# Two attention and mixer layers at decode: order of heads at the change of layer, the path from one layer's rows to the next layer's queries, and the end of the kernel

## The chip, the cores and the metric

One core of a Trainium2 chip runs the whole program; the other cores are idle. The metric is the device time of one execution in microseconds, as a median of several runs. A profiled execution of the same program gives the trace that the views below are taken from.

## The reference

Two sequences (B = 2), one new token each, of width D = 512. A layer is grouped-query attention over a cache of 32,768 keys with 32 query heads on 8 key and value heads of width 128, and then a mixer block whose MLP runs along the token axis (there is one token, so each of the 512 channels is sent through 1,792 hidden values by itself). Both are added to x after a LayerNorm. Two such layers follow each other, with the same weights and the same cache. All is float32.

```python
def _A_ref(x, k_cache, v_cache, wq, wo):
    q = (x @ wq).reshape(B, Sq, Hq, Dh).transpose(0, 2, 1, 3)
    k = jnp.repeat(k_cache, rep, axis=1)
    v = jnp.repeat(v_cache, rep, axis=1)
    scores = jnp.einsum("bhqd,bhkd->bhqk", q, k) * (Dh ** -0.5)
    p = _softmax(scores, axis=-1)
    o = jnp.einsum("bhqk,bhkd->bhqd", p, v)
    return o.transpose(0, 2, 1, 3).reshape(B, Sq, Hq * Dh) @ wo

def _B_ref(x, w1, b1, w2, b2):
    h = _layernorm(x, axis=-1)
    u = _gelu(jnp.einsum("bsd,sf->bdf", h, w1) + b1)
    y = jnp.einsum("bdf,fs->bds", u, w2) + b2
    return y.transpose(0, 2, 1)

x = x + _A_ref(_layernorm(x, axis=-1), A_k_cache, A_v_cache, A_wq, A_wo)
x = x + _B_ref(_layernorm(x, axis=-1), B_w1, B_b1, B_w2, B_b2)
# and the same two lines once more
```

The second layer's queries for a sequence need that sequence's first layer to be complete: all eight heads, the output projection, the mixer and a LayerNorm. Its keys and values are those of the first layer again.

## The kernel before

A unit is one layer, sequence and key head, (layer, b, h). There are 32 units, each with 64 cells of K and 64 of V. A cell is a tile of 128 partitions by 512 floats, 256 KiB. The on-chip buffer `mem` holds 105 cells (`CELLS`), so nearly everything is streamed, and the two layers stream the same cache twice. Work goes in steps of four cells. A K step runs eight matmuls (two per cell in float32) into score tiles in PSUM (`k_step`, line 315); a V step runs eight matmuls into `acc` (`v_step`, line 366).

Class `Order` (line 41) writes down the order of all K and V steps. In the steady part it is K of one unit and then V of the unit before, so that the softmax of a unit is done while V of its predecessor passes. At each of the two changes of layer (one per sequence) stand three units: x, the last head of layer 0 for that sequence; fill, a unit of the other sequence that keeps the machine busy while the mixer of x's sequence is worked out; and y, the same head as x in layer 1, which needs its result. The order there is K of x, V of the unit before, first half of K of fill, V of x, second half of K of fill, V of fill, K of y, V of y. Because y reads the same cache as x, 64 V cells and 8 K cells of x are kept on chip for y (`KEPT_V`, `KEPT_K`). With 16 cells of weights for the two heads concerned, 17 cells are left for streaming during that time.

`plan_loads` (line 112) plans all loads ahead of time with a model of the queue and of TensorE (`CELL_US`, `LAND_US`, `LEAD_US`, `STEP_US`, and the `us` of the hooks): for each load it takes the largest of 32, 24, 16, 8 or 4 cells that makes the queue wait least, and a place in `mem`. `Order.cut` fixes sizes by hand: four-cell loads for the second half of fill's K and for all of fill's V, a taper (16, 8, 4, 4) at the end of x's V, and (16, 8, 4, 2, 1, 1) at the end of the last unit's V. All loads are issued from SP (line 722), each waiting until the last matmul that reads its cells has ended.

Everything else hangs on steps: `at(p, f, ...)` (line 627) runs f behind step p, in the order of TensorE's queue. For each unit these are the maximum of the scores (`max_1`, `max_2`), the transposes and exponentials, the denominators, `take_out` (copy `acc` to SBUF), `out_1` (sum the four row groups and divide) and `out_2` (output projection into `rows`). When a sequence's last unit of a layer has passed, the mixer follows: `mix_1` (broadcast x into PSUM), `take_rows`, `mix_2` (add the attention output, LayerNorm statistics), `hidden_tiles` in eight turns (two Gelu tiles on ScalarE and the projection of the two before), `take_rows`, `mix_4` (add the mixer output, statistics of the next LayerNorm), `to_columns` (line 535) and the queries of y in three pieces (`make_q`). At a change this chain runs from one step behind x's V to 22 steps behind it, and K of y begins two steps later.

The last unit has its own end, `last_mixer` (line 547): its last two cells (`THIN`) go to `acc` by thin matmuls that need no summing over row groups, and the mixer's Gelu runs as three direct tiles and then groups of 3, 3, 3 and 2 tiles, whose affine part VectorE has made. The output leaves in four transfers, two each from SP and ScalarE.

## Time and profile before

| | |
|---|---|
| median of 3 runs | 2521.4 us (2520.32 to 2522.16) |
| the profiled execution | 2520.16 us, span 2518.4 us |
| mean granted TensorE clock | 0.753 of full speed |
| TensorE busy with matmuls | 1442.3 us (57% of the span) |
| VectorE, ScalarE | 181.3 us, 183.7 us (7% each) |
| DMA | 1066.71 MB, 424 GB/s on the mean, 236 transfers issued from SP, most of 1, 2, 4 and 8 MB |

The page of the profile gives the busy time of each engine, a row of 40 slices of the span with the rate of the DMA engines, and the chain of work that ended last, followed back from the end. `SPq` is SP's queue of DMA issues. In the rows of windows the columns are the stretch, its length, busy time and number of instructions of PE (TensorE matmul), PEld (weight loads), DVE (VectorE), ACT (ScalarE) and POOL (GpSimd), then the granted clock of TensorE as a part of full speed, the busy share of the DMA engines and GB/s. In rows of the timeline they are start, duration, engine, line, operation, output <- input, shapes and count; in brackets stands the idle time before, and what ended it.

### The profile page before, as it was taken

How to read it: one execution, taken by the hardware profiler on the slowest of the kernel's cores; microseconds unless marked ns; L12 is line 12 of the kernel's file. 1: busy time of each engine (PE TensorE's matmuls, PEld its weight loads, DVE VectorE, ACT ScalarE, POOL GpSimd, SP SyncE). 2: the span in 40 equal slices, each digit the busy share in tenths (PEclk: the TensorE clock that was granted, in tenths of full speed). 3: DMA queues.
4: the chain of work that ended last, by engine and by line, in shares of the span. 5: the costliest groups of instructions: out<-in, count | busy, mean ns of one | idle time of the engine just before them, and what ended most of it. 6: DMA issues, size and time to landing. Idle time of an engine off the chain costs nothing.

```text
span 2518.4 us, 20745 instructions
## 1 busy us (share of the span) xinstructions
PE 1442.3 (57%) x9484; PEld 400.0 (16%) x9484; DVE 181.3 (7%) x473; ACT 183.7 (7%) x572; POOL 4.9 (0%) x16
## 2 busy tenths in 40 slices
...
GB/s 416 432 436 434 434 431 432 431 431 431 431 433 433 433 435 433 418 435 396 403 427 398 397 425 430 438 434 431 431 433 433 434 430 438 434 426 433 426 430 258
DMA packets 33792, 1066.71 MB, mean 424 GB/s; under 512 B 4005, under 2 KB 4009, under 8 KB 4394
## 3 DMA queue, kind: packets, MB, share of 16 engines
...
q10 hardware_dynamic: 6, 0.00, 0.0%
HBM read 1065.38 MB, written 0.00 MB: 423 GB/s over the span
## 4 chain that ended last, share of the span: by engine, by line
DMA 67%; PE 31%; ACT 1%; DVE 1%; issue 0%; SPq 0%; POOLq 0%; ACTq 0%; DVEq 0%
DMA mem<-in_kt_dram 36%; DMA mem<-in_v_dram 30%; PE acc L375 12%; PE scores L322 12%; PE misc L420 2%; PE rows L437 2%; PE misc L289 1%; ACT S L357 0%; PE rows L493 0%; PE misc L346 0%; PE misc L340 0%; PE bcast L457 0%; PE acc L592 0%; PE misc L539 0%; PE bcast L519 0%
## 5 line engine op out<-in xcount | busy, mean ns | idle before, releaser
L375 PE MATMUL acc<-mem,S 128*16 128x512 f32 x4092 | 626.7, 711 | 523.0 <-DMA mem<-in_v_dram 513.3
L322 PE MATMUL scores<-mem,qz 128*32 128x512 f32 x4096 | 613.4, 734 | 524.9 <-DMA mem<-in_kt_dram 524.8
L357 ACT ACTIVATE S<-S,neg 128x128 f32<-128x128 f32 x256 | 129.6, 509 | 2247.1 <-DVE S L352 1180.9
L322 PEld LDWEIGHTS scores<-mem,qz 128*32 128x32 f32 x4096 | 136.8, 128 | 926.0 <-DMA mem<-in_kt_dram 469.2
L375 PEld LDWEIGHTS acc<-mem,S 128*16 128x16 f32 x4092 | 129.9, 106 | 848.3 <-issue 793.1
L332 DVE TENSOR_REDUCE mx<-scores 128x1 f32<-128x512 f32 x64 | 44.3, 692 | 827.9 <-PE scores L322 827.9
L289 PE MATMUL misc<-mem,xn 128*2 128x512 f32 (+1 forms) x144 | 86.9, 737 | 4.3 <-DMA mem<-in_wqo_dram 4.3
L420 PEld LDWEIGHTS misc<-selg,row 128*128 128x128 f32 x256 | 50.8, 295 | 46.8 <-issue 41.6
L352 DVE STREAM_TRANSPOSE S<-scores 128x512 f32<-128x512 f32 x64 | 45.5, 711 | 140.7 <-PE acc L375 140.7
L420 PE MATMUL misc<-selg,row 128*128 128x4 f32 x256 | 53.6, 333 | 0.6 <-DVE row L405 0.6
L437 PE MATMUL rows<-mem,oT 128*1 128x512 f32 x248 | 52.1, 931 | 0.0
L357 ACT ACTIVATION_READ_ACCUMULATOR S<-S,neg 128x1 f32 x256 | 47.7, 187 | 0.0
L493 PE MATMUL rows<-hid,cols_sb 128*1 128x512 f32 x84 | 33.8, 616 | 1.0 <-ACT hid L508 1.0
L342 DVE TENSOR_REDUCE m<-misc 1x4 f32<-1x128 f32 x32 | 8.9, 278 | 342.4 <-PE misc L340 342.4
L415 DVE COPY row<-acc 128x512 f32<-128x512 f32 x31 | 21.5, 692 | 149.7 <-PE acc L375 149.7
L508 ACT ACTIVATE hid<-bcast,bias,scale 128x512 f32<-128x512 f32 x42 | 30.4, 774 | 17.0 <-PE rows L493 8.6
L289 PEld LDWEIGHTS misc<-mem,xn 128*2 128x2 f32 (+1 forms) x144 | 14.5, 101 | 74.2 <-issue 72.9
L428 DVE TENSOR_TENSOR oT<-misc,rl 128x4 f32<-128x4 f32 x32 | 5.2, 162 | 283.6 <-PE misc L420 283.6
L294 DVE COPY row<-misc 2x512 f32<-2x512 f32 (+1 forms) x18 | 12.2, 679 | 183.5 <-PE misc L289 123.0
L340 PE MATMUL misc<-ident,mxa 128*1 128x128 f32 x64 | 17.8, 375 | 5.1 <-DVE mxa L338 5.1
L401 DVE RECIPROCAL rl<-misc 128x4 f32<-128x4 f32 x32 | 5.9, 183 | 197.4 <-PE misc L399 197.4
L298 PEld LDWEIGHTS misc<-ident,row 2*128 2x128 f32 (+1 forms) x144 | 17.3, 186 | 16.2 <-issue 12.7
...
## 6 DMA issues: line engine op xcount, KB each, us to landing
mem<-in_kt_dram SPq DMA_DIRECT2D x27, 2048.0 KB, 13.0
...
mem<-in_wqo_dram SPq DMA_DIRECT2D x14, 2048.0 KB, 33.1
...
mem<-in_v_dram SPq DMA_DIRECT2D x8, 2048.0 KB, 10.4
...
```

Of the source, the lines that this page charges most:

```text
L289: nc.tensor.matmul(q_ps[us][:n, :], xn[layer][:, d, b : b + n], wq[:, d, :], start=(d == 0), stop=(d == DT - 1))
L322: nc.tensor.matmul(sc_ps[u, half][32 * row : 32 * row + 32, :], qz[:, at : at + 32], cells(at_cell["K", u, g], 1), start=(i == 0), stop=(i ...
L332: nc.vector.tensor_reduce(mx[u][:, half : half + 1], sc_ps[u, half], axis=AX.X, op=ALU.max)
L340: nc.tensor.matmul(pm[:1, :P], mxa, ident, start=True, stop=True)
L352: nc.vector.transpose(S[half], sc_ps[u, half])
L357: nc.scalar.activation(s[:, :, h], s[:, :, h], AF.Exp, bias=neg[u][:, h : h + 1], scale=SCALE, accum_out=lsum[u][:, half, h : h + 1],)
L375: nc.tensor.matmul(acc[32 * row : 32 * row + R * QT, :], S[half][:, col : col + R * QT], vc, start=(g < NG), stop=(g >= quads - NG),)
L415: nc.vector.tensor_copy(asb[u], acc)
L420: nc.tensor.matmul(po[:, :R], asb[u][:, t * DH : (t + 1) * DH], selg[:, t * R : (t + 1) * R], start=(t == 0), stop=(t == QT - 1),)
L437: nc.tensor.matmul(rows[b][32 * r : 32 * r + 1, :], oT[u][:, r : r + 1], wo_of(u)[:, r, :], start=(u == order.first_of[layer, b]), stop=(u ...
L493: nc.tensor.matmul(rows[key[1]][32 * g : 32 * g + 1, :], w2c[:, f : f + 1], hid.pop((key, f)), start=(f < NG), stop=(f >= FT - NG),)
L508: nc.scalar.activation(hid[key, f], px[key], AF.Gelu_apprx_tanh, bias=shift[key][:, f : f + 1], scale=slope[key][:, f : f + 1],)
```

## The change

The order at a change becomes K of x, V of the unit before, all of K of fill, V of x, V of fill, K of y, V of y. Ten K cells are kept instead of eight, and `mem` has 106 cells; the room comes from the second buffer of `hidden`, whose place the row tile takes for every other hidden tile. The planner's constants for landing and lead are 1.1 and 1.8 us.

The chain from x's V to y's queries is rewritten for the 16 steps of fill's V. `mix_1` runs two steps before V of x ends, `out_1` and `out_2` directly behind it. `half_way` turns the rows of the attention into columns while the mixer runs, and `change_1` adds the columns of the mixer's rows. The queries are computed from x without its LayerNorm, beside a second row that holds the column sums of the weights; the mean and the deviation come from two all-partition sums, and `change_2` applies both with a pair of factors in the small matmuls that turn the queries into columns. `mix_4`'s copy and statistics and `to_columns` go.

At the end of the kernel eight cells are thin instead of two, and they go to a PSUM tile of their own, so that `take_out` and the summing of the row groups (`out_sum`) run before the last four cells. `last_rows` puts what is known of the rows into PSUM before the last V starts, where the denominators, the row copy and `mix_1` now stand as well. The two halves of the last projection lie in different PSUM tiles, copied out by VectorE and ScalarE; one broadcast and one `bn_stats` follow. The last Gelu groups are 3, 3, 3, 1, 1, and the output leaves in one transfer. The first half of the last unit's V is loaded in two pieces. At the start, x and the small columns are loaded from ScalarE's queue instead of SP's.

```diff
-CELLS = 105
+CELLS = 106
 WCELLS = 8
-KEPT_K = 8
+KEPT_K = 10
 KEPT_V = 64
 SIZES = (32, 24, 16, 8, 4)
 FINAL = (16, 8, 4, 2, 1, 1)
 TAPER = (16, 8, 4, 4)
-THIN = 2
+THIN = 8
 SLOTS = 4
 DIRECT = 3
-TAIL_GROUPS = (3, 3, 3, 2)
-TAIL_CELLS = 16
+TAIL_GROUPS = (3, 3, 3, 1, 1)
+TAIL_CELLS = 18
 EPS = 1e-5
 
 LOAD_US = 0.12
 CELL_US = 0.6024
-LAND_US = 1.0
-LEAD_US = 2.5
+LAND_US = 1.1
+LEAD_US = 1.8
 STEP_US = 1.44
...
-        self.k(x0), self.v(before[-1]), self.k(fill0, 0), self.v(x0), self.k(fill0, 1), self.v(fill0)
-        self.k(y0), self.v(y0), self.k(x1), self.k(fill1, 0), self.v(x1), self.k(fill1, 1), self.v(fill1)
+        self.k(x0), self.v(before[-1]), self.k(fill0), self.v(x0), self.v(fill0)
+        self.k(y0), self.v(y0), self.k(x1), self.k(fill1), self.v(x1), self.v(fill1)
         self.k(y1), self.v(y1), self.k(n)
...
-        for x, fill, _ in self.changes:
+        for x, fill, y in self.changes:
+            self.cut("K", y, KEPT_K, (-KEPT_K % STEP,))
             self.cut("V", x, HALF, TAPER)
-            self.cut("K", fill, HALF, (STEP,) * 8)
             self.cut("V", fill, 0, (STEP,) * 16)
+        self.cut("V", self.last, 0, (HALF // 2, HALF // 2))
         self.cut("V", self.last, HALF, FINAL)
...
-    hidden = ctx.enter_context(tc.tile_pool(name="hidden", bufs=2))
+    hidden = ctx.enter_context(tc.tile_pool(name="hidden", bufs=1))
...
-    nc.sync.dma_start(xcols, x)
+    nc.scalar.dma_start(xcols, x)
...
-                    acc[32 * t : 32 * t + R, :DH],
+                    thin[32 * t : 32 * t + R, :DH],
                     S[half][:, col + t * R : col + (t + 1) * R],
                     vc[:, t * DH : (t + 1) * DH],
-                    start=False,
-                    stop=True,
-                    skip_group_check=True,
+                    start=(g == quads),
+                    stop=(g == 2 * HALF - 1),
...
+    thin = rows[0]
+    po_of = {}
+
+    def out_sum(u):
+        po_of[u] = pmisc.tile([P, G], F32, name="misc")
         for t in range(QT):
             nc.tensor.matmul(
-                po[:, :R],
+                po_of[u][:, :R],
                 asb[u][:, t * DH : (t + 1) * DH],
                 selg[:, t * R : (t + 1) * R],
                 start=(t == 0),
-                stop=(t == QT - 1),
-            )
+                stop=(t == QT - 1 and u != order.last),
+            )
+
+    def out_1(u):
+        if u == order.last:
+            nc.tensor.matmul(po_of[u][:, :R], asb["thin"], selg[:, :R], start=False, stop=True)
+        else:
+            out_sum(u)
+        po = po_of[u]
...
-                hid[key, f] = hidden.tile([P, D], F32, name="hid")
+                hid[key, f] = hidden.tile([P, D], F32, name="hid") if f % 2 else row_tile()
...
+    def all_sum(dst, src):
+        p = pmisc.tile([P, G], F32, name="misc")
+        nc.tensor.matmul(p[:, :DT], ones, src, start=True, stop=True)
+        nc.vector.tensor_reduce(dst, p[:, :DT], axis=AX.X, op=ALU.add)
+
+    def columns(key):
         pt = pmisc.tile([P, G], F32, name="misc")
         for d in range(DT):
             nc.tensor.matmul(
-                pt[:, d : d + 1], ysb[key][:, d * P : (d + 1) * P], ident[:, :1], start=True, stop=True
-            )
-        xT[b] = const.tile([P, DT], F32, name=f"xT_{b}")
-        nc.vector.tensor_scalar_add(xT[b], pt[:, :DT], b2c)
-        mv, rs = stats[key]
-        nc.vector.tensor_scalar(xn[1][:, :, b], pt[:, :DT], mv[:, 0:1], rs, op0=ALU.subtract, op1=ALU.mult)
+                pt[:, d : d + 1], ysb[key][:, d * P : (d + 1) * P], selg[:, 0:1], start=True, stop=True
+            )
+        return pt[:, :DT]
+
+    def half_way(key):
+        nc.vector.scalar_tensor_tensor(sq, columns(key), b2c, xT[key[1]], op0=ALU.add, op1=ALU.add)
+
+    def change_1(key, y):
+        b = key[1]
+        x = xq[b][:, :, 0]
+        wq = wq_sb[0, y[2]]
+        nc.vector.tensor_add(x, columns(key), sq)
+        xT[b] = x
+        q_ps[y] = pfix.tile([P, G], F32, name="bcast")
+        for d in range(DT):
+            nc.tensor.matmul(q_ps[y][:2, :], xq[b][:, d, :], wq[:, d, :], start=(d == 0), stop=(d == DT - 1))
+        all_sum(negm, x)
+        nc.vector.tensor_scalar_mul(negm, negm, -1.0 / D)
+        nc.vector.tensor_scalar_add(xn[1][:, :, b], x, negm)
+        nc.vector.tensor_mul(sq, xn[1][:, :, b], xn[1][:, :, b])
+        q_row[y] = row_tile()
+        nc.scalar.activation(q_row[y][:2, :], q_ps[y][:2, :], AF.Copy)
+
+    def change_2(key, y):
+        b = key[1]
+        all_sum(spread, sq)
+        nc.vector.tensor_scalar(spread, spread, 1.0 / D, EPS, op0=ALU.mult, op1=ALU.add)
+        nc.gpsimd.tensor_tensor(spread, spread, half_neg, op=ALU.pow)
+        nc.vector.scalar_tensor_tensor(
+            pair, ident[:2, 1:2], negm[:2, :], ident[:2, 0:1], op0=ALU.mult, op1=ALU.add
+        )
+        nc.vector.tensor_scalar_mul(pair, pair, spread[:2, :])
+        pt = pmisc.tile([P, G], F32, name="misc")
+        for r in range(R):
+            nc.tensor.matmul(
+                pt[:, r : r + 1], q_row[y][:2, r * DH : (r + 1) * DH], pair, start=True, stop=True
+            )
+        q_out((y,), pt)
+        nc.vector.tensor_scalar_mul(xn[1][:, :, b], xn[1][:, :, b], spread)
+
+    rest = [None, None]
+
+    def last_rows(u):
+        layer, b, h = u
+        key = (layer, b)
+        y = ysb[key]
+        nc.tensor.matmul(px[key], sel1, y, start=False, stop=False, skip_group_check=True)
+        for g in range(NG):
+            to = rows[b][32 * g : 32 * g + 1, :P]
+            nc.tensor.matmul(to, xT[b][:, g : g + 1], ident, start=True, stop=False, skip_group_check=True)
+            nc.tensor.matmul(
+                to, selg[:, 0:1], y[:, g * P : (g + 1) * P], start=False, stop=False, skip_group_check=True
+            )
+        for k in range(2):
+            rest[k] = pscore.tile([P, G], F32, name="scores")
+            nc.vector.memset(rest[k][:, : D // 2], 0.0)
...
     def last_mixer(u):
...
+        tiles = [cells(tail_at + k, 1) for k in range(TAIL_CELLS)]
+        flat, y, few = tiles[FT + 1], tiles[FT + 2], tiles[FT + 3][:, :DH]
         p = px[key]
-        st = work.tile([P, 2, 6], F32, name="ln_st2", bufs=1)
+        st = work.tile([P, 6], F32, name="ln_st")
         mv = work.tile([P, 2], F32, name="ln_mv")
         rs = work.tile([P, 1], F32, name="ln_rs")
+        nc.vector.tensor_copy(few, thin[:, :DH])
+        asb["thin"] = few
+        out_1(u)
         for k in range(2):
             for r in range(R):
                 nc.tensor.matmul(
-                    rw[32 * r : 32 * r + 1, k * w : (k + 1) * w],
+                    rest[k][32 * r : 32 * r + 1, :w],
                     oT[u][:, r : r + 1],
                     wo_of(u)[:, r, k * w : (k + 1) * w],
-                    start=False,
+                    start=True,
                     stop=True,
-                    skip_group_check=True,
                 )
-        halves_copy(y, rw)
-        for k in range(2):
-            c = slice(k * w, (k + 1) * w)
-            nc.tensor.matmul(p[:, c], sel1, y[:, c], start=False, stop=True, skip_group_check=True)
-            nc.vector.bn_stats(st[:, k, :], p[:, c])
-        res = acc[:, :P]
+        nc.vector.tensor_copy(y[:, :w], rest[0][:, :w])
+        nc.scalar.activation(y[:, w:], rest[1][:, :w], AF.Copy)
+        nc.tensor.matmul(p, sel1, y, start=False, stop=True, skip_group_check=True)
+        nc.vector.bn_stats(st, p)
+        res = rows[b][:, :P]
         for g in range(NG):
-            c = slice(g * P, (g + 1) * P)
-            to = acc[32 * g : 32 * g + 1, :P]
-            nc.tensor.matmul(to, xT[b][:, g : g + 1], ident, start=True, stop=False, skip_group_check=True)
-            nc.tensor.matmul(to, selg[:, 0:1], y[:, c], start=False, stop=False, skip_group_check=True)
+            nc.tensor.matmul(
+                rows[b][32 * g : 32 * g + 1, :P],
+                selg[:, 0:1],
+                y[:, g * P : (g + 1) * P],
+                start=False,
+                stop=False,
+                skip_group_check=True,
+            )
...
-        for g in range(NG):
-            (nc.sync if g % 2 else nc.scalar).dma_start(
-                out[b : b + 1, g * P : (g + 1) * P], o[32 * g : 32 * g + 1, :]
-            )
+        nc.sync.dma_start(out[b : b + 1, :].rearrange("o (g c) -> (o g) c", g=NG), o[0 : P : P // NG, :])
...
-        at(v_mid + 2, denominators, u, us=0.2)
-        at(v_end, take_out, u)
+        at(v0 - 1 if u == order.last else v_mid + 2, denominators, u, us=0.4)
         if u == order.last:
-            at(v_mid + 4, gelu_table)
-            at(v_mid + 3, mix_1, key, us=0.8)
-            at(v_end, out_1, u)
+            at(v0 - 1, take_rows, key)
+            at(v0 - 1, table, AF.Gelu_apprx_tanh)
+            at(v0 - 1, mix_1, key)
+            at(v0 - 1, last_rows, u)
+            at(v_end - 2, take_out, u)
+            at(v_end - 1, out_sum, u)
             at(v_end, last_mixer, u)
             continue
-        at(v_end + 1, out_1, u, us=1.0)
-        at(v_end + 2, out_2, u, us=2.4)
-        if u == order.last_of[key]:
-            e = v_end
-            at(e + 1, mix_1, key, us=0.8)
-            at(e + 3, take_rows, key)
-            at(e + 4, mix_2, key, us=0.7)
-            g0 = e + 9
-            for k in range(FT // 2 + 1):
-                at(g0 + k, hidden_tiles, key, k, us=1.0)
-            g0 += FT // 2
-            at(g0 + 1, take_rows, key)
-            at(g0 + 2, mix_4, key, us=0.7)
-            if layer == 0:
-                at(g0 + 3, to_columns, key, us=0.5)
-                (y,) = [y for y, (x, _) in changed.items() if x == u]
-                queries((y,), g0 + 4, g0 + 5, g0 + 6)
-                assert g0 + 6 < first["K", y]
+        at(v_end, take_out, u)
+        if u != order.last_of[key]:
+            late = 0 if u == order.v_before[order.last] else 1
+            at(v_end + late, out_1, u, us=1.2)
+            at(v_end + 2 * late, out_2, u, us=2.0)
+            continue
+        e = v_end
+        at(e - 2, mix_1, key, us=1.2)
+        at(e, out_1, u, us=1.9)
+        at(e + 1, out_2, u, us=2.0)
+        at(e + 1, take_rows, key)
+        at(e + 2, mix_2, key, us=1.2)
+        if layer == 0:
+            at(e + 2, half_way, key, us=1.0)
+        at(e + 2, table, AF.Gelu_apprx_tanh)
+        for k in range(FT // 2 + 1):
+            at(e + 4 + k, hidden_tiles, key, k, us=1.2)
+        e += 4 + FT // 2
+        at(e, take_rows, key)
+        at(e, table, AF.Exp)
+        if layer == 1:
+            at(e + 1, mix_4, key, us=1.2)
+            continue
+        (y,) = [y for y, (x, _) in changed.items() if x == u]
+        at(e + 1, change_1, key, y, us=2.8)
+        at(e + 2, change_2, key, y, us=0.8)
+        assert e + 2 < first["K", y]
...
-        load(label, n, a)
-    nc.sync.dma_start(cols_sb, cols)
-    for label, n, a in begin.get(-1, ())[1:]:
+    nc.scalar.dma_start(cols_sb, cols)
+    for label, n, a in begin.get(-1, ()):
         load(label, n, a)
```

61 lines of the change are left out of this document (22 added, 39 removed).

## Prediction

> **What bounds the kernel now.** I read the page first: slices, chain, issues.
>
> ```profile
> span 2518.4 us, 20745 instructions
> GB/s 416 432 436 434 434 431 432 431 431 431 431 433 433 433 435 433 418 435 396 403 427 398 397 425 430 438 434 431 431 433 433 434 430 438 434 426 433 426 430 258
> DMA 67%; PE 31%; ACT 1%; DVE 1%; issue 0%; SPq 0%; POOLq 0%; ACTq 0%; DVEq 0%
> mem<-in_kt_dram SPq DMA_DIRECT2D x27, 2048.0 KB, 13.0
> ```
>
> The chain is DMA, with TensorE only finishing what has just landed. The stream runs at 430 to 438 GB/s nearly everywhere, so bytes set the time, except at both ends and in two dips, the changes of layer (slices 19, 20 and 22, 23). Next the busy time by stretch.
>
> ```profile
> 500.00:1000.00 500.00, 263.88 (x1732) 72.88 (x1733) 29.81 (x77) 25.32 (x96) 0.00 (x0) 0.73 1.00 432
> 1160.00:1220.00 60.00, 48.64 (x267) 12.29 (x260) 8.69 (x24) 16.84 (x32) 1.09 (x2) 0.80 0.98 385
> 1220.00:1260.00 40.00, 20.69 (x137) 4.39 (x136) 3.39 (x8) 1.32 (x5) 0.00 (x0) 0.82 1.00 409
> 1360.00:1420.00 60.00, 47.77 (x258) 11.72 (x254) 8.00 (x24) 16.84 (x32) 1.08 (x2) 0.79 0.96 376
> 1420.00:1460.00 40.00, 26.22 (x148) 5.45 (x140) 3.68 (x9) 0.20 (x1) 0.00 (x0) 0.66 1.00 414
> 1192.00:1204.00 12.00, 7.86 (x45) 1.36 (x42) 2.37 (x6) 4.18 (x5) 0.00 (x0) 1.00 1.01 425
> ```
>
> The last column is GB/s, the third from last the granted clock. Against 432, the first change loses 60 x (1 - 385/432) = 6.5 us while fill's V passes and 40 x (1 - 409/432) = 2.1 in the K behind it; the second loses 7.8 and 1.7. There some 17 of the 105 cells are free (72 are kept, 16 hold weights), so loads of four cells wait until TensorE frees four. Fed without gaps (1192 to 1204) such loads make 425: the small size alone costs under 2%, the rest is starvation.
>
> The timeline there shows what held TensorE, and the unit prices.
>
> ```profile
> 1174.33 0.69 DVE L332 TENSOR_REDUCE mx<-scores 128x1 f32<-128x512 f32 x1 [6.09 <-PE scores L322]
> 1179.26 3.62 PE L375 MATMUL acc<-mem,S 128*16 128x512 f32 x16 [2.46 <-ACT S L357]
> ...
> 1166.99 5.29 DMA mem<-in_kt_dram
> ...
> 1186.56 1.45 ACT L508 ACTIVATE hid<-bcast,bias,scale 128x512 f32<-128x512 f32 x2 [0.44 <-PE rows L493]
> ...
> 1188.45 1.45 ACT L508 ACTIVATE hid<-bcast,bias,scale 128x512 f32<-128x512 f32 x2 [0.44 <-PE rows L493]
> ...
> 1200.10 1.05 PE L375 MATMUL acc<-mem,S 128*16 128x512 f32 x8 [1.34 <-DMA mem<-in_v_dram]
> 1201.09 1.12 PE L519 MATMUL bcast<-row,selg 128*128 128x512 f32 x2
> 1202.25 0.69 DVE L525 COPY row<-bcast 128x512 f32<-128x512 f32 x1 [4.42 <-PE bcast L519]
> 1204.03 0.54 POOL L532 TENSOR_TENSOR ln_rs<-ln_rs,half_neg 128x1 f32<-128x1 f32 x1 [36.33 <-DVE both L398]
> 1204.17 0.39 PE L399 MATMUL misc<-both,one 128*128 128x4 f32 x2 [1.96 <-DVE both L398]
> 1204.48 1.91 PE L375 MATMUL acc<-mem,S 128*16 128x512 f32 x8
> ...
> 1219.44 1.05 PE L420 MATMUL misc<-selg,row 128*128 128x4 f32 x8
> 1221.30 1.04 PE L437 MATMUL rows<-mem,oT 128*1 128x512 f32 x8
> ...
> 1160.88 1.93 PE L437 MATMUL rows<-mem,oT 128*1 128x512 f32 x8
> ```
>
> Fill's softmax stands between its last K and its first V: 4.9 us (1174.33 to 1179.26) in which no cell comes free. Its K is split around x's V, so nothing covers it. The same eight matmuls take 1.05 us or 1.91: TensorE at full and at half clock.
>
> **The change, part by part.**
>
> *Bytes.* Two more K cells stay per change, four of 262,144 B: 1.049 MB at 432 GB/s, -2.4.
>
> *Start.*
>
> ```profile
> 0.74 0.41 SPq L218 DMA_DIRECT2D xcols<-in_x_dram  x1
> 1.20 0.42 SPq L715 DMA_DIRECT2D mem<-in_wqo_dram  x1
> ...
> 28.56 4.50 PE L322 MATMUL scores<-mem,qz 128*32 128x512 f32 x20 [12.08 <-DMA mem<-in_kt_dram]
> ```
>
> With x on ScalarE's queue the first big load goes at 0.74: -0.5. x and cols may come a microsecond or two later; the wait of 12.1 us for the first K hides that, and without it they would cost just that.
>
> *The stage of fill's V, per change.* With all of fill's K ahead of x's V, its softmax runs under x's V: the 4.9 us go. But the mixer, spread over 24 steps of four cells until now, must fit in 16 steps of V, with queries due before step 17. What is late next is either the load or TensorE. Loads: 16 x 1.049 MB at 425 GB/s = 39.5 us. TensorE at full clock: 16 steps of 1.05 = 16.8; eight turns of hidden tiles, 1.89 each from one ACT row to the next where a step alone is 1.05, +6.7; and the chain in new form: take_out's copy and eight matmuls 0.69 + 1.05, out_2 1.04, row copy and mix_2 0.69 + 1.12, half_way 1.05, row copy and columns 0.69 + 1.05, queries 1.04 (L437 has their shape), two all-partition sums at 0.39, pow 0.54 and four small DVE steps of some 0.15 (estimate, 1.9 together), change_2's eight small matmuls 1.05: 11.4. Sum 34.9. At half clock the steps are 30.6 and the chain, with six of its groups at half rate (+0.86 to 0.89 each), 16.6: 53.9. How much TensorE may lag: sixteen free cells are four loads, 9.9 us; a load needs 5.3 from issue to use on a short queue (the DMA row at 1166.99) and 1.05 to be used, so 3.5 is spare. Starvation starts beyond 43.0. At the 0.80 granted now, two fifths of the way from full to half, TensorE needs 42.5: nothing on the whole. But the work is bunched. Out_1 to half_way with three steps is 8.8 (14.0 at half clock), at 0.80 10.9, against three loads and the spare, 10.9: nothing. Columns, queries, sums and change_2 with two steps are 7.8 (12.1), at 0.80 9.5, against 8.4: 1.1. The four-cell size costs 39.5 - 38.8 = 0.7. So 1.8 remains per change where 6.5 and 7.8 stand: -10.7. Bounds: 0.7 per change at full clock (-12.9); 53.9 - 43.0 + 0.7 = 11.6 at half clock (+8.9). I take the middle because 1192 to 1204, hidden tiles and waits on loads in turn, held clock 1.00, while 1204.48 fell to half behind a chain on VectorE.
>
> Change_1 and change_2 put waits into TensorE's order: behind its matmuls stand fill's V steps, and behind these SP's next loads; that is the 1.1 above. The Exp and Gelu table loads move to where ScalarE is idle; nothing.
>
> *The K behind it.* 10 kept cells instead of 8, a ring of 26 cells against 25, a first load of two cells, retuned planner constants. The rows show 2.1 and 1.7 lost; I leave both. Bounds: -3.8 if all goes, +3.8 if it doubles, since the sizes the planner chooses can be read from no row.
>
> *Elsewhere.* A lead of 1.8 us instead of 2.5 asks loads to start closer to their deadline; a 2 MB load now takes 13.0 from issue to landing, 4.9 of it its own transfer, so 8 covers the 0.7.
>
> *Tail.*
>
> ```profile
> 2476.54 1.91 PE L375 MATMUL acc<-mem,S 128*16 128x512 f32 x8 [14.57 <-DMA mem<-in_v_dram]
> ...
> 2493.32 4.04 PE L375 MATMUL acc<-mem,S 128*16 128x512 f32 x34
> ...
> 2497.62 0.61 PE L384 MATMUL acc<-mem,S 128*4 128x128 f32 x12
> 2498.31 0.42 DVE L405 COPY row<-acc 128x256 f32<-128x256 f32 x1 [6.77 <-PE acc L384]
> 2498.79 1.06 PE L420 MATMUL misc<-selg,row 128*128 128x4 f32 x8 [0.56 <-DVE row L405]
> 2501.74 0.39 ACT L406 ACTIVATE row<-rows 128x256 f32<-128x256 f32 x1 [2.58 <-DVE row L405]
> 2501.76 1.22 PE L570 MATMUL bcast<-row,selg 128*128 128x256 f32 x2 [0.61 <-DVE row L405]
> 2504.82 0.43 DVE L571 BATCH_NORM_STATS2 ln_st<-bcast 128x6 f32<-128x256 f32 x1 [1.38 <-PE bcast L570]
> 2509.08 5.16 ACT L613 ACTIVATE mem<-mem 128x1536 f32<-128x1536 f32 x4
> 2515.89 0.63 SPq L621 DMA_DIRECT2D out_dram<-mem  x2
> ```
>
> The last unit's denominators, row copy, mix_1 and last_rows move ahead of its V, where TensorE must now also sit out its exponentials: behind them stand its V steps. Until now TensorE waited 14.6 us there for one load of 32 cells (2476.54). Two loads of 16 end that wait 9.7 us sooner (16 x 0.262 MB at 432 GB/s), so some 5 are left over the new work; past that, 64 cells at two matmuls of 0.12 (34 in 4.04) are 15 us of TensorE against 39 of loads, which takes up the rest. Nothing.
>
> The last V matmul ends at 2498.2. Six more cells go thin, eight matmuls of 0.05 each (twelve in 0.61) where a row cell needs two of 0.12 (estimate): +1.0; out_sum's 1.05 ahead of the last four cells is paid by denominators and mix_1, which leave this place. So V ends 1.0 later (bounds -1.2, since half of this unit's V now comes in two loads and TensorE starts earlier, and +4 if it is at half clock). Then: a thin copy and two matmuls instead of 0.42 + 1.06, -0.8; one broadcast of 1.12 and one bn_stats of 0.70 instead of two halves in turn, 2501.76 to 2505.25, -1.6 (only -1.2 if the ACT half still waits for the DVE half, as at 2501.74); a last group of one tile, -0.2; one output transfer, not two in turn on a queue, -0.3. Sum -1.9, bounds -4 and +3.2.
>
> **Sum.** -2.4 - 0.5 - 10.7 - 1.9 = -15.5. The profiled execution took 2520.2 (span 2518.4 and 1.8 around it); 1.2 on top leads to the median of the runs, 2521.4. So 2504.7 in the profile, 2505.9 as a median.
>
> **Rivals.**
>
> 1. *TensorE at half clock (slower).* Between loads it idles, and its work in the fill's stage rises to 53.9 us: +8.9 for both changes; the tail's V end comes 4 later and its matmuls at half clock take back the rest, +3.2. With -2.4 and -0.5 that is +9.2: 2530.6. It decides below a granted clock of about 0.6 in the stage, where four fifths of the way to half make 50.1 and the loss 50.1 - 43.0 + 0.7 = 7.8, as much as now. For: 0.66 in 1420 to 1460, and 1204.48. Against: 0.80 and 0.79 in the stages themselves. The Trainium skill, "TensorE: Matmul & The Clock Gate", Part 1, has the clock fall after an idle window of about 3.4 us. By that rule waits of 1.3 us for loads leave it full; the trace disagrees, with half rate at 1204.48 after 1.96 us idle. Chance 0.17.
>
> 2. *The ring holds three loads, not four.* Ten kept cells are no multiple of four; if the planner leaves holes of two, 12 of 16 free cells serve. The spare of 3.5 falls to 1.0, and the bunches at 0.80 cost 10.9 - 8.4 = 2.5 and 9.5 - 5.9 = 3.6, with 0.7 that is 6.8 per change: -0.7 for both instead of -10.7. Total -5.5: 2515.9. No row shows a place in memory; 17 cells in fours left one over until now. Chance 0.18.
>
> 3. *Full clock all through.* 0.7 per change: 2.2 below the forecast, 2503.7. This is what the clock rule named above gives. If the K stage's 3.8 also go and the tail gives 4, 2497.8. For: 1.00 in 1192 to 1204. Chance 0.13.
>
> **Numbers.** My forecast has 0.52. Range 2498 to 2520: the best bound to beyond rival 2, leaving out mainly rival 1. A measurement here tells about 0.2% apart, 5.0 us: faster means under 2516.4. Forecast, rival 3 and the half of rival 2 below that are faster, 0.74; the other half of rival 2 same, 0.09; rival 1 slower, 0.17.
>
> **What would show it.** Right: no wait for the fill's softmax ahead of its V, slices at the changes above 420 GB/s, load gaps in the fill's V only around its last three steps, bytes down by 1.05 MB, first big load at 0.74, one bn_stats in the tail. Wrong: queries late for y's K, SP waiting on TensorE throughout the 16 steps, a granted clock under 0.6 there, or V matmuls at half clock at the very end.

## The result

| | before | changed |
|---|---|---|
| median | 2522.1 us (13 runs, 2517.6 to 2525.6) | 2517.2 us (13 runs, 2511.4 to 2520.5) |
| ratio to before | | 0.9978, 95% interval 0.9968 to 0.9987 |
| profiled execution, span | 2520.2, 2518.4 us | 2518.0, 2516.3 us |

The change makes the kernel about 4.9 us faster, 0.2%, where 15.5 had been forecast. Single executions of the changed kernel scatter over 9 us, so the two profiles, 2.1 us apart, show where the time went better than how much of it there is. First the page of the changed kernel: span, the rates of the 40 slices and the chain.

```profile
span 2516.3 us, 20894 instructions
...
GB/s 417 429 432 432 431 433 433 433 431 434 427 433 430 434 431 432 417 434 421 390 425 425 394 423 438 433 431 434 433 432 432 431 432 427 434 434 433 432 426 238
...
DMA 73%; PE 26%; issue 0%; ACT 0%; DVE 0%; POOL 0%; SPq 0%; POOLq 0%
```

DMA still bounds the kernel. The dips at the changes of layer have become narrower (one slice each, 390 and 394, instead of two each), but not shallower; the second slice lost 3 GB/s, the third and the last but one 4 each. The windows of the changed kernel:

```profile
60.00:120.00 60.00, 30.84 (x204) 8.71 (x204) 2.42 (x7) 4.24 (x16) 0.00 (x0) 0.72 0.99 421
1160.00:1220.00 60.00, 52.52 (x340) 15.02 (x332) 8.20 (x30) 18.05 (x35) 1.09 (x2) 0.91 0.94 388
1220.00:1260.00 40.00, 23.91 (x152) 5.53 (x152) 3.60 (x9) 3.55 (x15) 0.00 (x0) 0.78 1.01 418
1360.00:1420.00 60.00, 48.34 (x346) 14.66 (x334) 8.41 (x30) 18.04 (x35) 1.08 (x2) 1.00 0.96 396
1420.00:1460.00 40.00, 25.90 (x140) 4.65 (x144) 3.22 (x7) 4.14 (x16) 0.00 (x0) 0.66 0.99 407
2440.00:2495.00 55.00, 35.82 (x294) 12.38 (x286) 4.58 (x12) 5.71 (x18) 0.00 (x0) 0.81 0.91 375
```

and two windows of the kernel before that the prediction does not show:

```profile
60.00:120.00 60.00, 26.91 (x192) 7.95 (x193) 2.42 (x7) 4.23 (x16) 0.00 (x0) 0.69 1.01 436
2440.00:2495.00 55.00, 34.82 (x250) 10.19 (x252) 3.93 (x12) 6.99 (x19) 0.00 (x0) 0.78 0.98 420
```

By the prediction's own reckoning against 432 GB/s the stages of fill's V lose 6.1 and 5.0 us, where 6.5 and 7.8 stood and 1.8 each was forecast, although the granted clock was 0.91 and 1.00. And two places that the prediction gave nothing got worse: the start (421 instead of 436) and the end of the stream (375 instead of 420).

To put the whole span together I work out a loss from the packet records of the loads: in each stretch the time in which the 16 DMA engines had nothing to do, plus what the packets took beyond 2.418 us per 64 KB, the time of an undisturbed one. What is left of the time up to the last landing is the stream at full rate; the tail is the time from the last landing to the end of the span. All in microseconds:

```
               loss in the stretch                                          at full
        0-120  120-1150  1150-1260  1260-1350  1350-1460  1460-2410  2410-end   rate   tail    span
before    3.7       6.6       10.3        1.9       10.9        7.6       2.4  2452.1   22.8  2518.4
changed   4.9       8.1        8.4        2.0        8.5        6.9       7.0  2449.6   21.1  2516.3
```

So -2.5 for the bytes, -4.3 at the two changes, -1.7 in the tail and -0.6 elsewhere, and on the other side +2.7 up to 1150 and +4.6 at the end of the stream (each figure is rounded). This is one execution of each kernel. How far such a figure moves from one execution to the next can be seen below: three kernels that end with the same code and the same loads as the changed one lose 5.5, 4.5 and 7.3 from 2410 on, so the mean of the four is +3.7.

**At a change of layer** the timeline of TensorE in the changed kernel shows the whole bunch, from the step of V ahead of the columns to the steps of V behind the small matmuls:

```profile
1204.94 1.05 PE L383 MATMUL acc<-mem,S 128*16 128x512 f32 x8 [0.52 <-DMA mem<-in_v_dram]
1205.92 1.05 PE L546 MATMUL misc<-selg,row 128*128 128x1 f32 x8
1207.32 3.59 PE L562 MATMUL bcast<-mem,xq 128*2 128x512 f32 x8 [0.35 <-DVE xq L558]
1210.84 0.39 PE L540 MATMUL misc<-xq,one 128*128 128x4 f32 x2
1211.15 1.05 PE L383 MATMUL acc<-mem,S 128*16 128x512 f32 x8
1212.22 0.36 PE L540 MATMUL misc<-sq,one 128*128 128x4 f32 x2
1213.97 1.02 PE L581 MATMUL misc<-pair,row 2*128 2x1 f32 x8 [1.39 <-DVE pair L578]
1214.92 4.46 PE L383 MATMUL acc<-mem,S 128*16 128x512 f32 x24
```

The bunch takes 10.0 us (1204.94 to 1214.92); 7.8 had been reckoned at full clock. The queries (L562) take 3.59 instead of 1.04. The sums and the two waits for VectorE are 2.4 of it (0.35, 0.31, 0.36 and 1.39); 2.6 had been reckoned (0.69 for the copy of the row and 1.9). Nothing waits for the softmax of fill any more. SP's issues in the same stretch:

```profile
1203.55 2.83 SPq L790 DMA_DIRECT2D mem<-in_v_dram  x2
1212.27 8.36 SPq L790 DMA_DIRECT2D mem<-in_kt_dram  x5
```

From 1206.4 to 1212.27 SP issues nothing, because the cells for the first load of y's K, one of two cells, come free behind the V step at 1211.15. The next load waits for the step at 1214.92 and leaves at 1216.55, with its first packet 1.0 us later: the queue had run dry, and no packet moved from 1215.6 to 1217.5.

**At the end of the stream** SP issues the last loads at these times: in the kernel before six, of 16, 8, 4, 2, 1 and 1 cells, and in the changed one the five from 8 cells down:

```profile
2462.04 2.70 SPq L722 DMA_DIRECT2D mem<-in_v_dram  x6
```

```profile
2478.38 12.16 SPq L790 DMA_DIRECT2D mem<-in_v_dram  x5
```

and the chain of the changed kernel shows that the stream and TensorE take turns there:

```profile
2462.78 20.81 DMA mem<-in_v_dram
2483.73 1.95 PE acc L383 x8
2485.69 7.37 DMA mem<-in_v_dram
2495.14 1.69 PE rows L392 x32
```

A load of four cells is issued at 2485.69 by the end of a V step that itself had waited for a load. In the kernel before, all of them had been issued by 2464.8.

**The tail** of the changed kernel (timeline):

```profile
2493.10 1.06 PE L392 MATMUL rows<-mem,S 128*4 128x128 f32 x32 [1.70 <-DMA mem<-in_v_dram]
...
2495.07 1.73 PE L392 MATMUL rows<-mem,S 128*4 128x128 f32 x32
...
2498.04 1.89 PE L619 MATMUL scores<-mem,oT 128*1 128x256 f32 x16 [0.25 <-DVE oT L437]
...
2500.43 2.08 PE L628 MATMUL bcast<-mem,selg 128*128 128x512 f32 x2 [0.50 <-ACT mem L627]
...
2513.53 0.64 SPq L680 DMA_DIRECT2D out_dram<-mem  x1
```

The last V matmul ends at 2496.8, 1.6 us behind the last landing (2495.24); in the kernel before it was 2.6 (2495.59 to 2498.2). But from 2495.29 on the granted clock is 0.5, and the sixteen matmuls of the projection take 1.89 where they took 1.04. The single output transfer is issued at 2513.53 and the span ends 2.8 us later; before, the first of the four was issued at 2515.89 and the end came 2.5 later. It saved nothing.

### The profile page after: what moved, and what is told of

The parts are those of the page before. It is cut to its first block, busy times and chain, and to the rows that moved or that the text cites. A ratio compares the mean times of both kernels' runs of the same rounds, so it can differ in the third digit from the quotient of the medians.

```text
span 2516.3 us, 20894 instructions
## 1 busy us (share of the span) xinstructions
PE 1430.8 (57%) x9550; PEld 400.0 (16%) x9550; DVE 181.2 (7%) x484; ACT 186.2 (7%) x580; POOL 5.0 (0%) x18
## 4 chain that ended last, share of the span: by engine, by line
DMA 73%; PE 26%; issue 0%; ACT 0%; DVE 0%; POOL 0%; SPq 0%; POOLq 0%
DMA mem<-in_kt_dram 37%; DMA mem<-in_v_dram 36%; PE acc L383 11%; PE scores L330 11%; PE misc L293 1%; PE misc L302 1%; PE misc L406 0%; PE bcast L562 0%; PE rows L502 0%; PE misc L422 0%; PE rows L652 0%; ACT S L365 0%; PE rows L392 0%; ACT mem L662 0%; PE bcast L628 0%
## 5 line engine op out<-in xcount | busy, mean ns | idle before, releaser
L383 PE MATMUL acc<-mem,S 128*16 128x512 f32 x4080 | 600.3, 696 | 525.8 <-DMA mem<-in_v_dram 520.9
L293 PE MATMUL misc<-mem,xn 128*2 128x512 f32 (+1 forms) x128 | 74.2, 712 | 1.8 <-issue 1.8
L437 DVE TENSOR_TENSOR oT<-misc,rl 128x4 f32<-128x4 f32 x32 | 5.2, 163 | 257.1 <-PE misc L422 256.4
L298 DVE COPY row<-misc 2x512 f32<-2x512 f32 (+1 forms) x16 | 10.9, 679 | 170.0 <-PE misc L293 109.5
L502 PE MATMUL rows<-row,cols_sb 128*1 128x512 f32 x42 | 22.3, 614 | 0.6 <-ACT row L517 0.6
L502 PE MATMUL rows<-hid,cols_sb 128*1 128x512 f32 x42 | 22.3, 613 | 0.0
L517 ACT ACTIVATE row<-bcast,bias,scale 128x512 f32<-128x512 f32 x21 | 16.3, 777 | 39.0 <-PE rows L502 20.2
L406 PEld LDWEIGHTS misc<-both,one 128*128 128x128 f32 x64 | 11.9, 232 | 40.5 <-issue 25.9
```

The lines of the kernel that those rows point to most:

```text
L293: nc.tensor.matmul(q_ps[us][:n, :], xn[layer][:, d, b : b + n], wq[:, d, :], start=(d == 0), stop=(d == DT - 1))
L383: nc.tensor.matmul(acc[32 * row : 32 * row + R * QT, :], S[half][:, col : col + R * QT], vc, start=(g < NG), stop=(g >= quads - NG),)
L502: nc.tensor.matmul(rows[key[1]][32 * g : 32 * g + 1, :], w2c[:, f : f + 1], hid.pop((key, f)), start=(f < NG), stop=(f >= FT - NG),)
L517: nc.scalar.activation(hid[key, f], px[key], AF.Gelu_apprx_tanh, bias=shift[key][:, f : f + 1], scale=slope[key][:, f : f + 1],)
```

## The experiments

Each kernel here is the changed one with the edit that is shown; the last three start from the kernel called "together". Each time is a median of five to seven runs, and each ratio is to the kernel before, timed beside it. Against the 0.9978 of the changed kernel, the ratios of the single edits that gain (0.9963 to 0.9967) have intervals that overlap with its own, so what one edit does is read mainly from where the losses lie, in one profile of each.

**Queries in four groups of rows.**

```diff
-        q_ps[y] = pfix.tile([P, G], F32, name="bcast")
+        q_ps[y] = px[key]
...
-            nc.tensor.matmul(q_ps[y][:2, :], xq[b][:, d, :], wq[:, d, :], start=(d == 0), stop=(d == DT - 1))
+            nc.tensor.matmul(q_ps[y][32 * d : 32 * d + 2, :], xq[b][:, d, :], wq[:, d, :], start=True, stop=True)
...
-            pair, ident[:2, 1:2], negm[:2, :], ident[:2, 0:1], op0=ALU.mult, op1=ALU.add
+            pair, selg[:, 1:2], negm, selg[:, 0:1], op0=ALU.mult, op1=ALU.add
```

> The queries at a change are computed into four groups of 32 rows (the part for feature tile d into rows 32d and 32d+1), and the small matmuls that turn them into columns add the four parts. Theory 1 (the queries were priced wrong: eight matmuls into the same two rows follow each other at 0.43 us, 3.59 us in all, while eight into four groups of rows take 1.04): the query matmuls fall from 3.59 to about 1.1 us, TensorE reaches the K of y and SP its loads about 2.5 us earlier, and the loss of DMA time in 1210 to 1225 and 1405 to 1420 (4.8 and 3.9 us, against 2.1 and 1.8 in the kernel before) falls by about 2 us each; time about 4 us less than the changed kernel, 2513. Rival A (the hops between TensorE, VectorE and GpSimd for the two sums and the power hold the array, however long the queries are): the queries get shorter, but the loads of y's K leave at the same time and the two losses stay; time within 1 us of the changed kernel, 2517. Rival B (the 3.59 us are those of the matmul's shape, not of the rows it writes): the queries still take 3.5 us.

Measured: 2515.9 us, ratio to before 0.9967 (0.9954 to 0.9980). The first bunch in its timeline:

```profile
1204.07 1.05 PE L383 MATMUL acc<-mem,S 128*16 128x512 f32 x8 [0.51 <-DMA mem<-in_v_dram]
1205.05 1.05 PE L546 MATMUL misc<-selg,row 128*128 128x1 f32 x8
1206.45 1.74 PE L562 MATMUL bcast<-mem,xq 128*2 128x512 f32 x8 [0.35 <-DVE xq L558]
...
1208.64 1.73 PE L383 MATMUL acc<-mem,S 128*16 128x512 f32 x8
...
1212.09 1.02 PE L581 MATMUL misc<-pair,row 128*128 128x1 f32 x8 [1.40 <-DVE pair L578]
```

At the second change the eight took 1.04; at the first they met a stretch of half clock (the next step of V has 1.73). So theory 1 is right on the price of the queries and rival B falls. But the bunch only shortens from 10.0 to 9.0 at the first change and to 8.2 at the second, because the wait for `pair` stays, and the stretches around the changes lose 8.2 and 8.2 instead of 8.4 and 8.5. Behind the second bunch, three steps of V run at half clock, which in the changed kernel took 2.77:

```profile
1409.74 5.29 PE L383 MATMUL acc<-mem,S 128*16 128x512 f32 x24
```

Rival A is right that this edit alone brings next to nothing, though not in its reason alone: the loads of y's K left 1.8 us earlier at the first change, and how much the half clock took back isn't separated here.

**The small matmuls one step later** (alone, and with the four groups).

```diff
         nc.vector.tensor_scalar_mul(pair, pair, spread[:2, :])
+
+    def change_3(key, y):
+        b = key[1]
         pt = pmisc.tile([P, G], F32, name="misc")
...
         at(e + 2, change_2, key, y, us=0.8)
+        at(e + 3, change_3, key, y)
```

> The small matmuls of change_2, with the copies behind them, are issued one step of V later than the sums, the power and the pair (a function change_3); the queries are as in the changed kernel, and the plan of loads is the same. What is left open by the queries in four groups of rows: there the queries fell from 3.59 to 1.74 us and the loads of y's K left 1.8 us earlier, but the loss in 1210 to 1225 and 1405 to 1420 only went from 4.8 and 3.9 to 3.7 and 4.2. Theory 1b (what holds the array is the whole bunch, from the columns to the last small matmul 10.0 us with two steps of V in it, of which the wait for pair, 1.4 us, is one part and the queries another): with a step of V under the wait for pair, the load of y's K that left at 1216.55 (its first packet 1 us later, so the queue was empty) leaves about 2.4 us earlier, and the loss in the two windows falls by 1 to 2 us each; time 2 to 3 us less than the changed kernel, 2514.5. Rival A (the loss there comes from the loads of 2 and 4 cells themselves and from places in memory that come free late, not from TensorE's order): the losses stay within 0.5 us.

> Both edits of the change's bunch at once: queries into four groups of rows, and the small matmuls of change_2 one step of V later. Theory 1b: the loss in 1210 to 1225 and 1405 to 1420 falls from 4.8 and 3.9 us to about 1.5 each, so that the stages of fill's V have what the prediction had forecast for them; time 5 us less than the changed kernel, 2512. Rival A: no less lost than with the hops apart alone.

Measured: alone 2512.9 us, 0.9963 (0.9951 to 0.9976); both 2510.6, 0.9951 (0.9939 to 0.9964). Alone, the wait for `pair` is gone but the queries, serial still, hit the half clock at the first change:

```profile
1207.68 5.29 PE L562 MATMUL bcast<-mem,xq 128*2 128x512 f32 x8 [0.35 <-DVE xq L558]
...
1216.03 1.02 PE L584 MATMUL misc<-pair,row 2*128 2x1 f32 x8 [0.41 <-DVE pair L578]
```

With both edits:

```profile
1204.07 1.05 PE L383 MATMUL acc<-mem,S 128*16 128x512 f32 x8 [0.51 <-DMA mem<-in_v_dram]
...
1206.45 1.04 PE L562 MATMUL bcast<-mem,xq 128*2 128x512 f32 x8 [0.35 <-DVE xq L558]
...
1209.53 1.05 PE L383 MATMUL acc<-mem,S 128*16 128x512 f32 x8 [0.37 <-DMA mem<-in_v_dram]
1210.56 1.02 PE L584 MATMUL misc<-pair,row 128*128 128x1 f32 x8
```

and its windows:

```profile
1160.00:1220.00 60.00, 50.31 (x360) 15.34 (x353) 8.60 (x31) 18.01 (x35) 1.08 (x2) 0.94 1.00 415
1220.00:1260.00 40.00, 26.09 (x164) 5.02 (x156) 3.39 (x8) 4.14 (x16) 0.00 (x0) 0.70 0.98 397
1360.00:1420.00 60.00, 48.32 (x354) 14.51 (x342) 7.76 (x30) 18.03 (x35) 1.08 (x2) 0.97 1.01 418
1420.00:1460.00 40.00, 24.80 (x160) 5.34 (x153) 3.22 (x7) 4.17 (x16) 0.00 (x0) 0.80 0.99 400
```

From the first of these steps to the end of the small matmuls it is 7.5 us with one step of V more in it, and in the middle TensorE waits for loads again: it is ahead of the stream. The loss in 1210 to 1225 and 1405 to 1420 is 1.3 and 0.8, where it is 4.8 and 3.9 in the changed kernel, 3.7 and 4.2 with the four groups alone, 5.1 and 3.1 with the step alone. By the prediction's reckoning the stages of fill's V lose 2.4 and 1.9, where 1.8 each was forecast. Not all of that is kept: the K behind them loses 3.2 and 3.0 instead of 1.3 and 2.3, so the whole stretches go from 8.4 and 8.5 to 6.5 and 6.4. Neither edit alone comes near this. A spare would act so: as long as the bunch is longer than what the loads in flight cover, shortening it partly leaves the queue empty all the same. But the half clock met both single edits (the queries and three steps of V above, and the queries of 5.29), so how much is the spare and how much the clock isn't shown. Theory 1b stands for the pair, with the queries as one of two parts. Of what it expected of the step alone, nothing came at the first change and 0.8 us at the second. The time that run gained is in its tail, 18.1 us, and at the end of the stream.

**The work ahead of the last V priced.**

```diff
-            at(v0 - 1, last_rows, u)
+            at(v0 - 1, last_rows, u, us=9.0)
```

> One number is added: the planner is told that the work ahead of the last unit's V costs 9 us. The plan of loads is the same up to the second load of 16 cells of that V; only the last six loads get other places in memory and are asked for behind the last step of the unit before, instead of behind steps of the last V itself. Theory 2 (the last loads wait for TensorE's steps of the last V, because the planner did not know what stands ahead of them): the load of 8 cells leaves at about 2463 instead of 2478, the DMA time lost between 2440 and 2500 falls from 11.6 to about 7 us, the last load lands 4 to 5 us earlier; time about 4.5 us less than the changed kernel, 2512.5. Rival: the last V is bound by TensorE itself, which starts it only at 2472 and has half clock there: the loads leave early, but the end moves by less than 1 us; 2517.

Measured: 2513.6 us, 0.9967 (0.9955 to 0.9979). The last five loads leave 17 us earlier, and the chain has one stretch of loads there:

```profile
2461.65 2.32 SPq L790 DMA_DIRECT2D mem<-in_v_dram  x5
```

```profile
2458.60 23.66 DMA mem<-in_v_dram
```

The loss from 2410 on falls from 7.0 to 4.2, which is 2.8 of the 4.6 that the change had added, and the last load lands 3.5 us earlier (2491.75). The waits of the last loads are gone, so theory 2 holds on what they waited for; by the rival the end would have moved by less than 1 us. The size is less sure: with the work unpriced the four kernels named above lose 4.5 to 7.3 there, and the smallest of these is close to 4.2.

**The old constants.**

```diff
-LAND_US = 1.1
-LEAD_US = 1.8
+LAND_US = 1.0
+LEAD_US = 2.5
```

> The planner's landing time and lead are those of the kernel before (1.0 and 2.5 us instead of 1.1 and 1.8), all else as changed. Theory 3 (the shorter lead opens small gaps in the stream that the prediction held to be covered): the load of K that left at 70.2 leaves at 56 again and the 1.4 us lost between 60 and 120 go, as does about 1 us between 1000 and 1080 and half of one elsewhere; time 2 to 3 us less than the changed kernel, 2514.5. Rival: queue depth hides the lead, and the loss at the start belongs to a hole in memory (cells 74 and up reused later), which no lead mends: within 1 us of 2517.

Measured: 2512.6 us, 0.9965 (0.9952 to 0.9978). SP's issues between 40 and 80 of the changed kernel, and of this one:

```profile
70.17 0.33 SPq L790 DMA_DIRECT2D mem<-in_kt_dram  x1
```

```profile
56.48 0.33 SPq L790 DMA_DIRECT2D mem<-in_kt_dram  x1
```

The load leaves 13.7 us earlier, and the loss up to 120 falls from 4.9 to 3.5. The gap was the constants' doing. Around 1000 to 1080 nothing came back (1.9 and 2.3). The larger part is again at the end, 7.0 to 3.2: the other constants give the load of eight cells a place that is free at 2460.9. Here the tail kept its clock (L619 1.04, L628 1.13) and took 19.1 us. Its thin matmuls waited only 0.25 us for a load, but that is not shown to be the reason: in the kernel with the work priced they waited for none, and the projection came at half clock:

```profile
2493.93 1.89 PE L619 MATMUL scores<-mem,oT 128*1 128x256 f32 x16 [0.26 <-DVE oT L437]
```

**Fill's K split again,** in two plans.

```diff
-        self.k(x0), self.v(before[-1]), self.k(fill0), self.v(x0), self.v(fill0)
-        self.k(y0), self.v(y0), self.k(x1), self.k(fill1), self.v(x1), self.v(fill1)
+        self.k(x0), self.v(before[-1]), self.k(fill0, 0), self.v(x0), self.k(fill0, 1), self.v(fill0)
+        self.k(y0), self.v(y0), self.k(x1), self.k(fill1, 0), self.v(x1), self.k(fill1, 1), self.v(fill1)
...
+            self.cut("K", fill, HALF, (STEP,) * 8)
```

The second plan also has `KEPT_K = 8`, without the cut of y's K, and the old constants.

> Fill's K is split around x's V again as in the kernel before (its second half in loads of four cells behind x's V), all else as changed. Theory 4 (the order of K was worth what the prediction said: fill's softmax, 4.9 us at each change, is covered now): the loss of DMA time in 1150 to 1210 and 1350 to 1405 rises from 2.1 and 1.9 us to about 6 and 7, as in the kernel before, and the wait of TensorE for fill's exponentials ahead of its V is back; time about 9 us more than the changed kernel, 2526. Rival (the order is worth little, the two stages gained because half_way takes the work of the columns out of the chain and the hidden tiles and tables moved): time within 2 us of 2517, the losses there stay at about 2.

> The changed kernel with the old planner constants, eight kept K cells and fill's K split around x's V as in the kernel before. In the first try of the split the planner left only three places of four cells for the loads of fill's V, so that its loss (11.1 and 7.4 us in 1180 to 1210 and 1380 to 1405) mixes two causes; in this plan there are four places, as in the kernel before and in the changed one. To be compared with the run with the old constants (2512.6), which holds K together. Theory 4 (the order of K is worth what the prediction said): 2.4 us for the bytes, and 4 to 6 us more lost at each change, in the 30 us ahead of the bunch, where fill's softmax shows as a wait of TensorE: 2525. Rival (three places, not the softmax, made the loss of the first try): 2516, only the bytes and a microsecond more.

Measured: 2529.6 us, 1.0028 (1.0017 to 1.0039), and 2529.0, 1.0026 (1.0015 to 1.0037). The losses in 1150 to 1260 and 1350 to 1460 are 17.3 and 15.4 with three places, 16.7 and 16.1 with four, where the kernel with the old constants has 7.4 and 9.5. Against the changed kernel, from which the first plan differs by the split alone, that is 8.9 and 6.9 us more; the second differs from the kernel with the old constants by 9.3 and 6.6, and in the kept cells too. Both runs came out some 4 us slower than theory 4 had expected. So its direction holds. The number of places is not seen to matter, though the two plans differ in more than that. The stall of the softmax is back in the timeline of the second plan, and TensorE is at half clock behind it:

```profile
1180.68 1.91 PE L383 MATMUL acc<-mem,S 128*16 128x512 f32 x8 [3.68 <-ACT S L365]
```

More is lost than in the kernel before, which loses 10.3 and 10.9 in these stretches. The likely reason, not tested by itself, is that the chain now stands right behind that stall: its bunch comes at 1190 to 1200, in the middle of fill's V, onto a queue that has not recovered. So the 9.3 and 6.6 are not the price of the softmax alone.

**Together:** four groups, the small matmuls a step later, the priced work, the old constants.

> Four edits at once: queries in four groups of rows, small matmuls of change_2 a step later, 9 us told to the planner ahead of the last V, and the old landing time and lead. If the causes found so far are separate ones, the gains add up: against the changed kernel about -3 (constants), -3 (end of the stream), -4 (the two bunches), and -1 to -2 more where the clock holds through the tail: 2505 to 2507. If they share one cause (each run was only another placement of loads, with some 4 us of scatter), it is no better than the best of them alone, 2512.

Measured: 2504.4 us (2503.3 to 2507.9), ratio 0.9934 (0.9920 to 0.9947). Its windows:

```profile
1160.00:1220.00 60.00, 50.54 (x365) 15.09 (x354) 8.43 (x30) 18.06 (x35) 1.09 (x2) 0.94 1.01 416
...
1360.00:1420.00 60.00, 48.45 (x336) 14.54 (x328) 7.50 (x27) 15.86 (x27) 1.08 (x2) 0.94 1.01 416
```

The gains nearly add up: against the changed kernel the medians gained 6.6 (the pair of edits), 3.6 and 4.6, in sum 14.8, and 12.8 came. Stretch by stretch they don't: at the end of the stream the priced work and the old constants gain 2.8 and 3.8 alone and 3.2 together (they act on the same last loads), while the two changes lose 4.1 and 5.0 where the pair alone left 6.5 and 6.4. The stages of fill's V lose 2.2 us each by the same reckoning (60 x (1 - 416/432)), where the prediction had put 1.8.

**Three variants of that kernel:** the first half of the last V uncut, `KEPT_K = 8`, and `LEAD_US = 3.2`.

```diff
-        self.cut("V", self.last, 0, (HALF // 2, HALF // 2))
```

> The four edits together, but the first half of the last V comes in one load of 32 cells again, as in the kernel before. In the kernel with the four edits the second load of 16 is asked for at 2449.20 with an empty queue (first packet 1.01 us later), and 1440 to 2460 and what follows still lose 3.6 us where the kernel before lost 1.8. Theory 5 (the cut opens that gap, and covers nothing, because the time of TensorE at the end is set by the last cells): the loss from 2440 on falls to about 2 us; time 1.5 us less than 2504.4. Rival (what the prediction said of the cut: TensorE starts the last V 9.7 us sooner and needs that): V ends later after the last landing than the 1.0 us it takes now, time 2 us more.

> The four edits together, with eight kept K cells instead of ten. 1.05 MB more, which is 2.4 us; on the other side loads of 8 cells instead of 2 and 4 in the K behind fill's V, and no loads of 16, 4 and 2 for the rest of K's first half around 1010 to 1060, where the kernel with the four edits loses 2.5 us (1000 to 1080) and the one with eight kept cells and split K 1.3. If the bytes decide: 2 us more, 2506.5. If the shapes of the loads cost what the bytes bring: within 0.5 us of 2504.4.

> The four edits together, with a lead of 3.2 us instead of 2.5. If the gaps that are left (2.5 us in 1000 to 1080, 5.1 in 120 to 1000, 6.1 in 1550 to 2380) are loads asked for too close to their time, they shrink by 2 to 4 us in all: 2501.5. If they are the loads' own shapes and packets, only the placement changes: within 2 us of 2504.4, to either side.

Measured: 2503.2 us, 0.9926 (0.9913 to 0.9940); 2504.8, 0.9926 (0.9914 to 0.9939); 2507.5, 0.9936 (0.9923 to 0.9948). The losses of all these, as above:

```
                 0-120  120-1150  1150-1260  1260-1350  1350-1460  1460-2410  2410-end   rate   tail    span
changed            4.9       8.1        8.4        2.0        8.5        6.9       7.0  2449.6   21.1  2516.3
q_four_rows        4.6       7.4        8.2        2.0        8.2        6.8       5.5  2449.6   22.6  2514.9
hops_apart         4.6       8.4        9.7        1.3        8.2        8.8       4.5  2449.6   18.1  2513.2
four_rows_apart    4.9       7.6        6.5        1.2        6.4        7.3       7.3  2449.5   18.2  2508.9
end_priced         4.6       7.5        7.4        2.4        8.3        7.9       4.2  2449.5   20.1  2511.9
old_constants      3.5       7.5        7.4        2.5        9.5        7.1       3.2  2449.6   19.1  2509.4
together           3.5       8.0        4.1        1.5        5.0        7.1       3.8  2449.4   19.1  2501.5
together_uncut     3.5       8.0        3.6        1.4        7.0        6.3       2.7  2449.5   19.4  2501.3
together_kept8     3.5       6.8        7.0        1.3        4.1        6.9       3.0  2452.0   18.4  2503.1
together_lead32    3.5       7.5        4.3        1.7        9.2        6.2       3.4  2449.3   19.7  2504.8
```

Uncut, the end loses 1.1 less and V still ends 1.1 us behind the last landing: the cut covered nothing (theory 5). In time it is within the scatter, and the second change loses 2.0 more. The two more kept cells save 2.6 us of bytes at full rate, and the losses are the same in sum within 0.4 (33.0 and 32.6), with more at the first change and less before and at the second with eight cells. The last load lands 2.3 us later with eight, as the bytes say, but the medians are only 0.4 apart: no more than that can be told. With the longer lead the long stretches lose 0.5 and 0.9 less and the second change 4.2 more, so there is no gain in time.

## Why the prediction was wrong

The forecast was 15.5 us and 4.9 came. By its steps:

- **Bytes** (-2.4): right, -2.5 at full rate. **Start** (-0.5): right, the first packet of the first big load goes at 1.78 instead of 2.25.
- **Stage of fill's V** (-10.7): wrong, -3.2 by its own windows. The first half was right: the softmax stall is gone, and of "the middle" and "half clock" for the clock it is nearly the full rate that came, 0.91 and 1.00. What failed is the step that sets "Columns, queries, sums and change_2 with two steps" at 7.8 us against a cover of 8.4: both sides were mis-sized. The bunch is 10.0 at full clock, and one price in it was wrong. "Queries 1.04 (L437 has their shape)" was 3.59: as many matmuls, as long, but L437's eight go to four groups of rows and these to one. The sums and hops to VectorE and GpSimd were priced about right, 2.4 against 2.6. The cover was shorter, since the second of the two loads that stand against it is of two cells with ten kept, 1.2 us instead of 2.5, which leaves 7.1; the prediction names that load, but only in the K behind. The price of the queries alone does not explain the loss: with it mended the second bunch took 8.2, less than the 8.4 though more than the 7.1, and with V at half clock behind it the stretch lost 8.2 where it had lost 8.5. With a step of V put under the wait for `pair` as well, the stages lose 2.4 and 1.9, and 2.2 each in "together", where the step had 1.8. The design did have room for this gain in the stage; the edit as it was made did not reach it.
- **The K behind it** (0): right in sum, -0.8 and +0.6 by the windows, well inside its bounds.
- **Elsewhere** (0, "8 covers the 0.7"): wrong. The lead does not shift a load by 0.7 us; it decides which place the planner takes. For the load at 70.17 it took cells that come free one step later, and that step is the first of the next unit's K and comes 14 us later. The start lost 1.4 by it. Of the 1.5 more that are lost from 120 to 1150 the old constants bring back 0.6; the rest is open.
- **The moved work ahead of the last V** ("Nothing"): wrong, and the largest miss besides the stage: +4.6 at the end of the stream in the profile, +3.7 as a mean of four kernels. The step set 39 us of loads against 15 of TensorE as if the loads ran by themselves. But the planner, which was told nothing of that work, gave the last five loads places in cells of the same V, so that each waited for TensorE. One number gives 2.8 of it back. The cut into two loads, which the step counted as a help, costs 1.1 in "together".
- **Tail** (-1.9): the sum was near, -1.7, by luck, from parts that were not. Behind the last landing V ends 1.0 earlier and not 1.0 later: a thin cell's matmuls take 0.033 us each (32 in 1.06), not 0.05, so eight thin cells cost no more than row cells. The half clock then takes back 0.85 in the projection and 0.95 in the broadcast; in the kernels where the clock held, the tail is 18.1 to 19.7 us, 3 to 4.7 less than before. The single output transfer is worth nothing, not 0.3.

**The rivals.** The first (half clock in the stage) did not come. The second (three places for loads) did not either: the loads of fill's V have four. Its smaller spare did come in another form, as the load of two cells that shortens the cover. The third had the clock right, and with the two mended parts its 2503.7 is what "together" reached; but that kernel has edits which the change has not, so this doesn't bear the rival out, and as a forecast of this edit it shares the wrong price of the queries. What happened, a bunch that is longer than its cover at full clock and last loads that wait for TensorE, was in none of them.

**What could have been read beforehand.** The groups of the kernel before had both prices, the queries' own line L289 among them:

```profile
L289 PE MATMUL misc<-mem,xn 128*2 128x512 f32 (+1 forms) x144 | 86.9, 737 | 4.3 <-DMA mem<-in_wqo_dram 4.3
...
L437 PE MATMUL rows<-mem,oT 128*1 128x512 f32 x248 | 52.1, 931 | 0.0
```

Busy time by count is 0.60 us per matmul in the first and 0.21 in the second (part of both at half clock), while the mean duration of one is larger in the second. The row of the queries, from the changed kernel and from the one with both edits of the bunch, shows it for the same matmuls, which differ in the rows they write:

```profile
L562 PE MATMUL bcast<-mem,xq 128*2 128x512 f32 x16 | 7.2, 591 | 0.7 <-DVE xq L558 0.7
```

```profile
L562 PE MATMUL bcast<-mem,xq 128*2 128x512 f32 x16 | 2.1, 591 | 0.7 <-DVE xq L558 0.7
```

One matmul takes 591 ns in both; sixteen of them occupy the engine for 7.2 or for 2.1 us. The Trainium skill, "TensorE: Matmul & The Clock Gate", Part 3 ("Packing small matmuls"), has outputs in different groups of 32 partitions run side by side in the array, with a gain of 2.38 for three groups; the 7.2 to 2.1 here, a factor of 3.4 for four, points the same way.

**What stays open.** Why 1000 to 1080 loses 1.9 to 2.9 us with ten kept cells (1.6 with the longer lead) and 1.1 to 1.6 in the kernels with eight was not taken apart: the loads of 16, 4 and 2 cells there and one that is issued late (in "together" at 1061.76, its first packet 1.1 us later) are the candidates. What share of the loss at a change the clock has, and what share the bunch against its cover, is open too. And which of the executions of the changed kernel, 2511 to 2520, had which part of the losses isn't known, since one of them was profiled.
